# Masks, identity and turning matrices made on the chip, one-pass mask products, products of zeros first, and a new stored order

## The chip, the cores and the metric

The kernel runs on one core of one Trainium2 chip. The metric is the time of one execution on the device in microseconds. Durations and waits come from one profiled execution.

## The reference

Two parts follow each other for 8 batches of 576 positions. The attention has 8 heads of 64 channels; it adds a pooled attention (q, k and v averaged over 4 neighbouring positions, 144 by 144 scores, each result repeated 4 times) and a local one (only positions less than 4 apart).

```python
q_d = q.reshape(B, H, Sd, factor, D).mean(axis=3)     # k_d, v_d alike
out_up = np.repeat(sm_attn(q_d, k_d, v_d), factor, axis=2)
mask = np.abs(pos[:, None] - pos[None, :]) < factor
scores = np.where(mask, scale * np.matmul(q, k.transpose(0, 1, 3, 2)), -1000000000.0)
out_local = np.matmul(softmax(scores), v)
x = out_up + out_local                                # (batch, 576, 512)

h = gelu_tanh(x @ w_in)                               # 512 -> 1024
u, v = h[..., :512], h[..., 512:]
v_n = (v - mean(v)) / np.sqrt(var(v) + 1e-06) * g_ln
v_s = np.einsum('ts,bsd->btd', w_sg, v_n) + b_sg[None, :, None]
out = x + (u * v_s) @ w_out
```

## The kernel before, in words

A **pair** g = 4b + p is two heads of batch b; there are 32. Everything is written as small **tasks** with short names, and one long text, ORDER (line 88), lists every task in the order in which its instructions are emitted, with the engine after a slash where there is a choice (V VectorE, A ScalarE, P GpSimd). Each engine and each DMA queue runs its own instructions strictly in that order; a task waits for the data that it reads and for the buffer that it writes. The figures beside the tasks in the code ({"T": 1.85} and such) were a planner's costs and have no effect when the kernel runs.

Buffers come from three stores (SIZES, line 195): "ps", 8 banks of PSUM; "X", 10 buffers; "R", 38 buffers. `place` (line 64) walks through ORDER and hands out the buffer that has been free longest; a task that takes a buffer waits on the chip for the last reader of its former content, which can be a store to memory.

The tasks of a pair, with their lines:
- lq, lk, lv, lw: loads of q, k, v for the pooled part and v for the local part (370 to 386), on the SP queue, one on ScalarE's.
- qs, ks, vs: sums over 4 neighbours (388 to 409). qs and ks write qd and kd.
- S (the first four pairs) or YS: the local scores. Ten windows of 64 keys for 58 queries, each a 64 by 64 product per head (line 424). For the first four pairs the mask is put in by TensorE: two products ident_sb x mask_sb (line 417) open the sum, the scores add to it. For the later pairs VectorE adds the mask (ma, mb, line 432). Y is the pooled scores (line 445).
- mx, my: maxima (454, 456, 466, 468); nx, ny: their negatives; ea, eb, ec: exponentials (484, 492); re, rc: 1/sum; np, nq: normalising (506, 509).
- T, U, t: the probabilities are transposed by products with turn_l and turn_p, permuted identities (lines 512, 521); pa, pb, pc, pe copy the result from PSUM (line 221, the copy helper).
- D: probabilities times v (573, 589); oe, od, xa, xb (554 to 596): the two parts are added into x. xh, xl, xc: x split into a high and a low part for one-pass float32r products (604 to 611).

A batch then has v, u (lines 691, 769: x times w_in), vg (GELU), vb, vp, vn (mean and variance, 721 to 740), vh, vl (split, line 760), s (the spatial product, line 769), sa, sm (bias and gate, 807, 814), gh, gl (split), o (w_out, line 769), oa (adds x) and os (store, line 848). In batch 0 v is cut by k into vk tasks. Tasks that begin with w load the weights (doubles, taken apart on the chip: wu, wq, wb, wt, wh, wl, lines 297 to 326). s0.0 is the first spatial product of batch 0; it needs vl0.0 to vl0.4 and all of w_sg (wlq).

Ahead of the tasks a few clears are emitted (line 269 to 273): qd and od on GpSimd, parts of pd on VectorE. One DMA, task **small** (line 276), brings 926 columns for 128 partitions: seven masks of 64 columns, the identity, the turning matrices and g_ln. S waits for it, and so do T, U, t, ma and the first s.

## Time and profile before

| | us |
|---|---|
| median of 3 runs | 572.92 (572.8 to 573.14) |
| the profiled execution, its own time | 573.11 |
| its span, first to last instruction | 571.3 |
| TensorE busy | 553.5 (97%), 6992 products |
| VectorE busy | 412.9 (72%) |
| ScalarE busy | 342.6 (60%) |
| GpSimd busy | 312.8 (55%) |
| read and written | 52.64 and 9.44 MB, 109 GB/s over the span |

A busy share is an average. What matters is in which stretch which engine is full, and which wait ends last there. A wait is listed under the task that waited and what released it. Records of one engine can overlap a little, so a sum of mean durations is somewhat more than the busy time.

### The profile page before, as it was taken

Reading aid. Unit: us, or ns where it says so; the run is one execution under the profiler, and the core shown is the slowest. Engines: PE = TensorE matmul, PEld = TensorE weight load, DVE = VectorE, ACT = ScalarE, POOL = GpSimd, SP = SyncE. Lnnn points to the kernel's source line nnn. Section 1 sums busy time; section 2 is a strip of 40 time slices with the busy share of each in tenths; the row PEclk is TensorE's granted clock in tenths of the full one; section 3 lists DMA queues with packets and bytes.
Section 4 is the critical chain, followed back from the end, with each engine's and each line's share of the span. In section 5 each row is a group of like instructions: output and inputs, shape, how many; then the busy total and the mean of one; then the engine's idle time right before and its main releaser. Section 6 shows DMA issues by size and latency. Waiting matters only on the chain.

```text
span 571.3 us, 17427 instructions
## 1 busy us (share of the span) xinstructions
PE 553.5 (97%) x6992; PEld 517.8 (91%) x6992; DVE 412.9 (72%) x908; ACT 342.6 (60%) x1242; POOL 312.8 (55%) x394
## 2 busy tenths in 40 slices
...
GB/s 304 328 229 374 126 205 177 158 64 86 101 24 58 106 138 102 166 3 17 142 184 204 44 3 142 136 168 1 89 23 97 165 44 1 22 1 2 84 0 104
DMA packets 30609, 63.21 MB, mean 111 GB/s; under 512 B 3520, under 2 KB 3776, under 8 KB 30528
## 3 DMA queue, kind: packets, MB, share of 16 engines
...
q8 instruction: 55, 0.90, 0.7%
q10 hardware_dynamic: 144, 0.30, 0.1%
q14 instruction: 26, 0.21, 0.1%
HBM read 52.64 MB, written 9.44 MB: 109 GB/s over the span
## 4 chain that ended last, share of the span: by engine, by line
PE 84%; DVE 5%; ACT 2%; issue 1%; DMA 1%; POOL 0%; DVEq 0%; ACTq 0%
PE ps L769 52%; PE ps L691 17%; PE ps L589 3%; PE ps L512 3%; PE ps L445 3%; PE ps L573 2%; PE ps L521 2%; PE ps L424 2%; DMA out_dram<-R 1%; DVE R L740 1%; DVE st L721 1%; DVE R L760 1%; DVE X L432 0%; DVE stats L456 0%; ACT R L221 0%
## 5 line engine op out<-in xcount | busy, mean ns | idle before, releaser
L769 PE MATMUL ps<-wsg_h,R 128*128 128x288 f32 x576 | 121.2, 298 | 0.0
L769 PE MATMUL ps<-X,weight_z 128*128 128x288 f32 x512 | 110.2, 297 | 0.0
L769 PE MATMUL ps<-R,weight_r 128*128 128x288 f32 x768 | 107.9, 297 | 1.7 <-DVE R L596 1.7
L769 PEld LDWEIGHTS ps<-R,weight_r 128*128 128x128 f32 x768 | 103.4, 188 | 2.7 <-DVE R L596 2.0
L484 ACT ACTIVATE X<-X,nb 128x64 f32<-128x64 f32 x280 | 93.5, 338 | 7.5 <-DVE nb L463 7.0
L691 PE MATMUL ps<-weight_y,X 128*128 128x512 f32 x320 | 96.7, 396 | 0.4 <-DVE R L221 0.2
L769 PEld LDWEIGHTS ps<-wsg_h,R 128*128 128x128 f32 x576 | 94.1, 188 | 0.6 <-DVE R L760 0.3
L769 PE MATMUL ps<-wsg_l,R 128*128 128x288 f32 x320 | 92.7, 296 | 0.0
L769 PEld LDWEIGHTS ps<-X,weight_z 128*128 128x128 f32 x512 | 84.5, 188 | 1.3 <-ACT R L703 0.3
L769 PE MATMUL ps<-R,weight_z 128*128 128x288 f32 x256 | 75.5, 295 | 0.0
L691 PEld LDWEIGHTS ps<-weight_y,X 128*128 128x128 f32 x320 | 58.2, 188 | 13.7 <-POOL R L319 1.3
L769 PEld LDWEIGHTS ps<-wsg_l,R 128*128 128x128 f32 x320 | 60.3, 189 | 0.0
L807 DVE SCALAR_TENSOR_TENSOR vs<-ps,small_sb,b_sb 128x288 f32<-128x288 f32 x64 | 32.3, 514 | 37.3 <-PE ps L769 35.8
L732 POOL TENSOR_TENSOR rs<-rs,nhalf 128x1 f32<-128x1 f32 (+1 forms) x40 | 25.0, 625 | 57.8 <-DVE rs L723 57.8
L484 ACT ACTIVATION_READ_ACCUMULATOR X<-X,nb 128x1 f32 x280 | 53.1, 190 | 0.0
L691 PE MATMUL ps<-weight_y,R 128*128 128x512 f32 x128 | 50.4, 394 | 1.1 <-issue 1.1
L814 POOL TENSOR_TENSOR R<-R,vs 128x288 f32<-128x288 f32 x25 | 22.0, 880 | 51.6 <-DVE vs L807 33.8
L408 POOL TENSOR_TENSOR pairs<-R 112x256 f32<-112x256 f32 x56 | 45.4, 811 | 7.2 <-DMA R<-in_v_dram 7.0
L221 ACT COPY R<-ps 128x464 f32<-128x464 f32 (+4 forms) x92 | 33.8, 407 | 25.7 <-PE ps L512 13.9
L788 ACT ACTIVATE R<-ps 128x288 f32<-128x288 f32 x64 | 24.8, 410 | 40.1 <-PE ps L769 38.3
L769 PEld LDWEIGHTS ps<-R,weight_z 128*128 128x128 f32 x256 | 48.2, 188 | 0.7
L221 ACT CAST R<-R 128x512 fp32r<-128x512 f32 (+2 forms) x38 | 24.5, 647 | 35.3 <-DVE R L814 12.6
...
## 6 DMA issues: line engine op xcount, KB each, us to landing
...
```

The costliest lines, as they stand in the source:

```text
L221: (nc.scalar.copy if e == "A" else ENG[e].tensor_copy)(**kw)
L408: ENG[e].tensor_tensor(out=pairs, in0=v[:, 0:2], in1=v[:, 2:4], op=ALU.add)
L445: nc.tensor.matmul(out=st["sdv"][n][os, cs], lhsT=qd2[par][hs, i * QC:i * QC + HD], rhs=st["kd"][hs, ks], start=True, stop=True)
L484: nc.scalar.activation(out=st["ms"][:, t, :], in_=src, func=AF.Exp, bias=st["nb"][:, t:t + 1], scale=scale, accum_out=sums[par][:, t:t + 1])
L512: nc.tensor.matmul(out=out, lhsT=st["ms"][0:LD, 2 * c:2 * c + 2, :], rhs=turn_l, is_transpose=True, start=True, stop=True)
L589: nc.tensor.matmul(out=o[i][hs, c * QB:(c + 1) * QB], lhsT=v[ks, c, hs], rhs=pt[ks, c, h ^ int(2 * c + i >= NA)], start=True, stop=True)
L691: nc.tensor.matmul(out=acc, lhsT=r32(l), rhs=r32(weights[f"y{k}"][:, 0, w]), start=(i == 0 and ks[0] == 0), stop=(i == len(ops) - 1 and ks ...
L732: nc.gpsimd.tensor_tensor(out=rs[0:n], in0=rs[0:n], in1=nhalf[0:n], op=ALU.pow)
L769: nc.tensor.matmul(out=acc[:, 0:HALF], lhsT=r32(l), rhs=r32(r), start=(first and n == 0), stop=(last and n == len(ops) - 1))
L788: nc.scalar.activation(out=us[i // 2][:, half(i)], in_=at["ps", "m", b, "u", i][:, 0:HALF], func=AF.Gelu_apprx_tanh)
L807: nc.vector.scalar_tensor_tensor(out=vsb[i], in0=at["ps", "m", b, "s", i][:, 0:HALF], scalar=g_sb[:, i // 2:i // 2 + 1], in1=b_sb[:, half( ...
L814: ENG[e].tensor_tensor(out=u[:, half(i)], in0=u[:, half(i)], in1=vsb[i], op=ALU.mult)
```

## The change

Six things change.
- small brings only g_ln (4 columns, task g). Masks, identity and turning matrices are made on the chip: cm (GpSimd, a clear and six selections by position), ci (GpSimd, a clear and one selection), cb (the inner mask copied four times), cl and cp (turning matrices copied out of the identity).
- cr writes a float32r copy of masks and identity into one R buffer, held until S3; the mask products of the first four pairs read it and are one-pass products. ma and mb read the float32 mask as before.
- Four tasks Z multiply od2[0] by itself into a PSUM bank: Z3 and Z1 (two products each) open the order on TensorE, Z2 (two) stands ahead of Y3 and Z0 (five) ahead of vk0.0. The first four see the cleared tile; by the time of Z2 and Z0 the tile holds results of od0. Nothing reads the bank.
- The clears of qd and od move from GpSimd to VectorE.
- S waits for cr, ma for cb, T for cl, U for cl and cp, t for cp, the first s for g, each instead of small.
- ORDER is a new one throughout, with other choices of engine for many tasks.

The diff; of ORDER (105 lines of it change) only the lines that the text speaks of.

```diff
-lk0/A lq0/S ks0/V qs0/V Y0 my0 ny0/A small S0 ec0 wy1 wuy1 lq1/S qs1/P wqy1/V wby1 wty1 mx0 wy0 lk1/S S1 ks1/P wqy0/A
-wby0 lk2 ks2/V mx1 lq2 qs2/P lq3 Y1 S2 my1 wuy0 wy3 wqy3/V nx0/A ea0 eb0 re0/V rc0 qs3/P ny1/V nx1/A ea1 wby3 mx2 ec1
-np0/P T0 nq0/P pa0/V U0 pb0/V pc0/V t0 pe0/V wz1 Y2 wty0 lk3 why1/V wqz1/V eb1 re1/V rc1 lk5 nq1/P wuz1 nx2/V ea2
...
-whq2/A ua0.0 vl0.0/V wlq2/V u0.1 ua0.1 vs6 YS7 ma7 vl0.4/V ec6 whr2/A ea6 qs8/P mb7 my7 mx7 ny7/A t5 s0.0 sa0.0 wbr0
...
-vg3.4 D17 oe17/A vb3.4 vp3.4 T18 lv19 pa18/A vn3.4 vh3.1/V ma20 mb20 mx20 o2.5 oa2.5 os2.2 lk25 vh3.3/A vl3.3/V od17
-nq18/V xa17 o2.6 lw24 vh3.4/V vl3.4/P eb19 u3.3 o2.0 u3.5 lk27 ea19 re19/V rc19 np19/P ua3.5 vh3.0/A ua3.3 vl3.0/V
...
+Z3 lq0/S cm cb/V Z1 lk1/S lk0/A ks0/V qs0/V ci cr/A S0 mx0 nx0/V ea0 lq1/S qs1/V Y0 my0 ny0/V ks1/P Y1 lq3 qs3/V lk2
+ks2/P S1 cl/V ec0 eb0 my1 mx1 nx1/V ny1/V ea1 cp/V ec1 re0/V lq2 qs2/P Y2 my2 lk3 wy2 wqy2/V rc0 nq0/P np0/P wby2 eb1
+lq4 qs4/V S2 mx2 nx2/A ea2 S3 ny2/V T0 pa0/V lk4 ks4/P ks3/P re1/V rc1 nq1/P np1/P wy0 wuy0 wqy0/A wuy2 wty2 U0 pb0/V
...
+od0 xa0 xb0 YS4 my4 T1 ma4 why2/V wly2/P wuz2 eb3 U1 pa1/V pb1/V mb4 pc1/V xh0/A lw1/S wly0/P wy1 wuy1 t1 Z2 pe1/A
...
+lk5 ks5/P xa1 Z0 lq6 nx4/A wqy3/A wby3 pb2/A pc2/V vk0.0 wz3 lw2 ec4 pe2/A wqz1/A wbz1 ea4 xb1 YS5 my5 eb4 np3/P U3
...
+vp0.4 vn0.4 u0.1 ua0.1 vl0.1/V vl0.2/V wlq2/V vh0.4/A vl0.4/V YS7 pe5/V whr1/A D4 wr2 wr0 lv6 vs6 ma7 mb7 mx7 ea6
+oe4/V my7 s0.0 sa0.0 eb6 re6/V s0.2 sm0.0/V ny7/V nx7/V ec7 eb7 wlr1/P sa0.2 lk12 lk11 lv8 rc6 nq6/P np6/P ea7 lq10
...
+xc4 v1.4 t8 pe8/V lq19 lq13 os0.3 va1.4/V t9 pe9/A ec10 ea10 re10/A wtr2 wur0 vj1.4 wqr0/V wbr0 v1.3 YS11 ma11 vp1.2
...
+ZEROS = (5, 2, 2, 2)
 SIZES = {"ps": 8, "X": 10, "R": 38}
...
-    small_sb = const.tile([P, 7 * KB + P + LD + 2 * QD + KT], F32, name="small_sb")
-    mask_sb = small_sb[:, 0:7 * KB].rearrange("p (t k) -> p t k", k=KB)
-    ident_sb = small_sb[:, 7 * KB:7 * KB + P]
-    turn_l = small_sb[0:LD, 7 * KB + P:7 * KB + P + LD]
-    turn_p = small_sb[0:QD, 7 * KB + P + LD:7 * KB + P + LD + 2 * QD].rearrange("p (i c) -> p i c", i=2)
-    g_sb = small_sb[:, 7 * KB + P + LD + 2 * QD:]
+    mask_sb = const.tile([P, 7, KB], F32, name="mask_sb")
+    ident_sb = const.tile([P, P], F32, name="ident_sb")
+    turn_l = const.tile([LD, LD], F32, name="turn_l")
+    turn_p = const.tile([QD, 2, QD], F32, name="turn_p")
+    g_sb = const.tile([P, KT], F32, name="g_sb")
...
     vs2 = [const.tile([P, HALF], F32, name=f"vs{i}") for i in range(2)]
     nc.vector.memset(nhalf, -0.5)
-    for t in qd2 + od2:
-        nc.gpsimd.memset(t, 0.0)
+    for t in od2 + qd2:
+        nc.vector.memset(t, 0.0)
...
-    add("small", {"S": 0.5}, lambda e: nc.sync.dma_start(out=small_sb, in_=small), mb=0.4)
+    def select(out, in_, step, base, rise, op, fill):
+        nc.gpsimd.affine_select(out=out, in_=in_, pattern=[[step, out.shape[-1]]], base=base, channel_multiplier=rise,
+                                compare_op=op, fill=fill)
+    def const_mask(e):
+        band = mask_sb[:, 1]
+        nc.gpsimd.memset(band, 0.0)
+        for h in range(2):
+            rows = band[h * KB:(h + 1) * KB]
+            select(rows, rows, 1, 0, -1, ALU.is_ge, NEG)
+            select(rows, rows, -1, 6, 1, ALU.is_ge, NEG)
+        select(mask_sb[:, 0], band, 1, -3, 0, ALU.is_ge, NEG)
+        select(mask_sb[:, 6], band, -1, S - QB * (NT - 1) + 2, 0, ALU.is_ge, NEG)
+    def const_ident(e):
+        nc.gpsimd.memset(ident_sb, 0.0)
+        select(ident_sb, ident_sb, -1, 0, 1, ALU.not_equal, 1.0)
+    def const_bands(e):
+        copy(e, out=mask_sb[:, 2:6], in_=mask_sb[:, 1:2].broadcast_to([P, 4, KB]))
+    early_c = {}
+    def const_round(e):
+        c = buf("R", "c", 0)
+        early_c["m"] = c[:, 0:7 * KB].rearrange("p (t k) -> p t k", k=KB)
+        early_c["i"] = c[:, 7 * KB:7 * KB + P]
+        copy(e, out=r32(early_c["m"]), in_=mask_sb)
+        copy(e, out=r32(early_c["i"]), in_=ident_sb)
+    def halves(n, rows):
+        return ident_sb[0:rows].rearrange("p (a q) -> p a q", a=2)[:, :, 0:n]
+    def const_turn_l(e):
+        copy(e, out=turn_l[:, 0:2 * QB].rearrange("p (a q) -> p a q", a=2), in_=halves(QB, LD))
+        copy(e, out=turn_l[:, 2 * QB:LD], in_=ident_sb[0:LD, QB:HD])
+    def const_turn_p(e):
+        copy(e, out=turn_p[:, 0, 0:2 * QC].rearrange("p (a q) -> p a q", a=2), in_=halves(QC, QD))
+        copy(e, out=turn_p[:, 1, 0:QC], in_=ident_sb[0:QD, HD:QD])
+        copy(e, out=turn_p[:, 1, QC:2 * QC], in_=ident_sb[0:QD, 0:QC])
+        copy(e, out=turn_p[:, :, 2 * QC:QD], in_=ident_sb[0:QD, QC:HD].rearrange("p (a q) -> p a q", a=1).broadcast_to([QD, 2, QD - 2 * QC]))
+    def zeros(i, n):
+        def emit(e):
+            z = buf("ps", "z", i)
+            for _ in range(n):
+                nc.tensor.matmul(out=z[:, 0:NT * QB // 2], lhsT=od2[0][:, 0:P], rhs=od2[0], start=True, stop=True)
+        return emit
+    for i, n in enumerate(ZEROS):
+        add(f"Z{i}", {"T": 0.48 * n}, zeros(i, n), takes=[("ps", "z", i)], gives=[("ps", "z", i)])
+    add("cm", {"P": 1.7}, const_mask)
+    add("ci", {"P": 0.5}, const_ident)
+    add("cb", {"A": 0.3, "V": 0.25}, const_bands, ["cm"])
+    add("cr", {"A": 0.7, "V": 0.5}, const_round, ["cb", "ci"], takes=[("R", "c", 0)])
+    add("cl", {"A": 0.3, "V": 0.25}, const_turn_l, ["ci"])
+    add("cp", {"A": 0.6, "V": 0.4}, const_turn_p, ["ci"])
+    add("g", {"S": 0.5}, lambda e: nc.sync.dma_start(out=g_sb, in_=small), mb=0.1)
...
             sp = [buf("ps", "s", g, i) for i in range(2)]
             if early:
                 for i in range(2):
-                    nc.tensor.matmul(out=sp[i][:, 0:NW[i] * KB], lhsT=ident_sb, rhs=mask_sb[:, MB[i]:MB[i] + NW[i], :],
+                    nc.tensor.matmul(out=sp[i][:, 0:NW[i] * KB], lhsT=r32(early_c["i"]), rhs=r32(early_c["m"])[:, MB[i]:MB[i] + NW[i]],
                                      start=True, stop=False, skip_group_check=True)
             for t in (0, 4, 1, 5, 2, 6, 3, 7, 8, 9) if early else (4, 5, 0, 6, 1, 7, 2, 8, 3, 9):
...
-        given = dict(takes=[("ps", "s", g, 0), ("ps", "s", g, 1)], gives=[("R", "q", g), ("R", "k", g)])
+        given = dict(takes=[("ps", "s", g, 0), ("ps", "s", g, 1)], gives=[("R", "q", g), ("R", "k", g)] + ([("R", "c", 0)] if early else []))
         if early:
-            add(N("S"), {"T": 1.85}, scores, [N("lq"), N("lk"), N("D", ahead), "small"], **given)
+            add(N("S"), {"T": 1.85}, scores, [N("lq"), N("lk"), N("D", ahead), "cr"], **given)
             add(N("Y"), {"T": 0.45}, scores_d, [N("qs"), N("ks")], **given_d)
             def both(e):
...
-            add(N("ma"), {"V": 0.35}, masked(0), [SN(), "small"], takes=[("X", "ms", g)], gives=[("ps", "s", g, 0)])
+            add(N("ma"), {"V": 0.35}, masked(0), [SN(), "cb"], takes=[("X", "ms", g)], gives=[("ps", "s", g, 0)])
         add(N("mx"), {"V": 0.95 if early else 0.8}, top, ([SN()] if early else [N("ma"), N("mb")]) + [N("nx", 2)])
...
-        add(N("T"), {"T": 0.44}, turn, [N("np"), "small"], takes=[("ps", "t", g, 1)], gives=[("X", "ms", g)])
-        add(N("U"), {"T": 0.42}, turn2, [N("np"), N("nq"), "small"], takes=[("ps", "t", g, 2)], gives=[("X", "ms", g)])
-        add(N("t"), {"T": 0.31}, turn3, [N("nq"), "small"], takes=[("ps", "t", g, 3)])
+        add(N("T"), {"T": 0.44}, turn, [N("np"), "cl"], takes=[("ps", "t", g, 1)], gives=[("X", "ms", g)])
+        add(N("U"), {"T": 0.42}, turn2, [N("np"), N("nq"), "cl", "cp"], takes=[("ps", "t", g, 2)], gives=[("X", "ms", g)])
+        add(N("t"), {"T": 0.31}, turn3, [N("nq"), "cp"], takes=[("ps", "t", g, 3)])
...
-            w = [f"wlq{s}" for s in range(NS)] + ["b", "small"] if first else []
+            w = [f"wlq{s}" for s in range(NS)] + ["b", "g"] if first else []
...
-    eye = np.eye(P, dtype=np.float32)
-    turns = [eye[:, i] for i in (np.r_[0:QB, HD:LD, QB:HD], np.r_[0:QC, HD:QD, QC:HD], np.r_[HD:QD, 0:QC, QC:HD])]
-    r = (np.arange(P) % KB)[:, None]
-    c = np.arange(KB)[None, :]
-    band = (c >= r) & (c <= r + 6)
-    first = band & (c >= 3)
-    last = band & (c < S - QB * (NT - 1) + 3)
-    m = np.stack([first, band, band, band, band, band, last], axis=1)
-    mask = np.where(m, 0.0, NEG).astype(np.float32)
...
-        "small": np.concatenate([mask.reshape(P, -1), eye] + turns + [g], axis=1),
+        "small": g,
```

More of the change, by code (lines that the diff above doesn't have):

```diff
@@ L99 @@
-vk3.1 ks6/V lq7 oe3/V od3 xa3 xb3 wlz3/V xh3/V ea5 re5/A xl3/P xc3 wlq0/P vk4.2 vk3.2 T4 wbz0 wtz0 U4 whq4/A t4 wlq4/V
-v0.0 v0.2 rc5 qs6/V wqr2/A pa4/A wbr2 nq5/P wq2 lw4 vg0.0 vb0.0 v0.4 vp0.0 lw5 wlz2/P pb4/A lw13 qs7/V pc4/A va0.4/A
-vj0.4 b wq1 pe4/A v0.1 whz0/A vg0.1 vb0.1 vp0.1 u0.6 vn0.0 wlz0/P lv6 wr3 wqr0/A v0.3 whq3/A vg0.3 vb0.3 vg0.2 vg0.4
-vb0.2 wqr1/A wlq3/P wbr1 vn0.1 vb0.4 u0.4 vp0.2 vn0.2 u0.7 wur2 ua0.4 ua0.6 wur1 np5/P vh0.1/A u0.5 ua0.5 vp0.3 vp0.4
-YS6 ma6 mb6 D4 oe4/A od4 vh0.2/A my6 lq8 xa4 mx6 xb4 vn0.4 whq1/A wlq1/V ny6/V vn0.3 T5 pa5/A vh0.0/A ua0.7 nx6/V U5
@@ new lines @@
+lk5 ks5/P xa1 Z0 lq6 nx4/A wqy3/A wby3 pb2/A pc2/V vk0.0 wz3 lw2 ec4 pe2/A wqz1/A wbz1 ea4 xb1 YS5 my5 eb4 np3/P U3
+ma5 mb5 mx5 T3 pa3/A wqz3/V xh1/V wtz2 wtz1 why1/A lv2 whz2/A wlz2/V t3 vk3.0 ny5/A ec5 xl1/V lv3 wuy3 wly1/V wty3 wz0
+D2 vk2.0 lw3 wr1 oe2/A od2 re4/A rc4 np4/P xa2 lq8 whz1/A vk1.0 vk2.1 nx5/A wqz0/A vk1.1 vk0.1 vk3.1 why3/A pb3/A wuz3
+pc3/A pe3/V qs6/P nq4/P lk6 g xb2 D3 wbz0 wbz3 wtz3 xh2/A xl2/V wuz0 vk1.2 xc2 wqr1/A wbr1 vk2.2 vk3.2 eb5 vk0.2 oe3/V
+od3 xa3 xb3 xc1 lw6 ks6/V YS6 ea5 re5/A wly3/P xh3/A xl3/V v0.1 whz3/A wlz3/V ma6 mb6 wtz0 whz0/A wlz0/P v0.2 vg0.2
```

185 lines of the change are left out of this document (92 added, 93 removed).

## The prediction

> **What bounds the kernel now.** I read first the waits of TensorE in the first 78 us, then the busy time of every engine in ten stretches cut where those waits change, then the chain of work in order of time.
>
> ```profile
> PE ps L445 <- DVE qd L391: 6.5, 1, 6.5
> PE ps L512 <- POOL X L506: 2.6, 3, 1.6
> PE ps L769 <- DVE R L596: 1.7, 1, 1.7
> ```
>
> These are the longest waits of TensorE over the span: total, times, longest. The largest is the start, 6.5 us until Y0 has its inputs. The L769 wait is the only one of them behind the first 78 us.
>
> ```profile
> 0.00:5.03 5.03, 0.00 (x0) 0.00 (x0) 0.39 (x3) 1.28 (x1) 1.16 (x8) 1.00 0.65 194
> 5.03:20.00 14.97, 11.74 (x192) 8.20 (x192) 12.56 (x29) 11.06 (x59) 9.02 (x12) 1.00 1.02 350
> 20.00:35.00 15.00, 13.02 (x393) 10.83 (x397) 14.64 (x39) 13.74 (x72) 12.09 (x11) 1.00 0.91 277
> 35.00:49.50 14.50, 12.99 (x266) 10.45 (x255) 12.92 (x27) 13.47 (x55) 11.52 (x14) 1.00 0.90 317
> 49.50:77.74 28.24, 27.75 (x327) 25.31 (x328) 27.29 (x57) 23.30 (x61) 21.71 (x22) 1.00 0.57 179
> 77.74:106.00 28.26, 28.26 (x404) 27.79 (x405) 25.47 (x54) 25.99 (x122) 22.82 (x26) 1.00 0.78 243
> 106.00:260.00 154.00, 154.00 (x2005) 144.20 (x2004) 114.45 (x259) 104.99 (x360) 88.21 (x123) 1.00 0.27 80
> 260.00:274.60 14.60, 14.18 (x192) 12.95 (x191) 10.62 (x22) 11.85 (x37) 4.17 (x8) 1.00 0.20 57
> 274.60:568.40 293.80, 291.56 (x3237) 278.03 (x3235) 194.54 (x425) 136.87 (x484) 142.08 (x175) 1.00 0.25 78
> 568.40:571.30 2.90, 0.00 (x0) 0.00 (x0) 0.00 (x0) 0.00 (x0) 0.00 (x0) 0.86 0.30 104
> ```
>
> The columns are the stretch, its length, then busy time of PE, PEld, DVE, ACT and POOL, the granted clock, the DMA share and GB/s. From 77.74 on TensorE is busy for all but 0.42 us (260 to 274.6) and 2.24 us (the next stretch: the L769 wait, and about 0.5 at the end for the last addition, which stays). So that part is TensorE's: 490.66 us with 488.0 us of work. Before 77.74 it idles 12.2 us (65.5 busy of 77.74), and there VectorE is the full engine: 67.4 us busy of the 72.7 us from 5.03 to 77.74, 27.29 of 28.24 in the last of these stretches.
>
> ```profile
> 76.49 1.21 DVE R L760
> 77.74 9.87 PE ps L769 x72
> ...
> 271.83 4.51 DMA out_dram<-R
> 276.94 6.63 PE ps L769 x48
> ```
>
> The chain says the same: at 77.74 the first spatial product of batch 0 (task s0.0) starts when VectorE ends vl0.4 (L760). Further on, a store of 4.51 us leads to the products at 276.94: the buffer of xa17 is freed by store os2.2, written just ahead of it in the order.
>
> So I write the time as **X + 488.0 + later stalls + 2.9 + 1.8**. X is the start of s0.0, 2.9 the tail behind the last addition (last stretch), 1.8 what lies around the span (573.11 profiled, 571.3 span). Before: 77.74 + 488.0 + 2.66 + 2.9 + 1.8 = 573.1. The profiled run lies 0.2 above the median of 572.92; what a measurement of this kernel can tell from no change is about 0.2%, 1.15 us.
>
> **The change: TensorE before X.** Counted from the two orders, as many tasks of each kind stand ahead of s0.0 on TensorE after as before, the four zero tasks apart.
>
> ```profile
> 6.50 1.33 PE L445 MATMUL ps<-kd,qd 64*64 64x144 f32 x16 [6.50 <-DVE qd L391]
> 7.76 2.50 PE L417 MATMUL ps<-small_sb 128*128 128x256 f32 x4
> 10.19 1.14 PE L424 MATMUL ps<-R,R 64*64 64x64 f32 x40
> 11.26 1.34 PE L417 MATMUL ps<-small_sb 128*128 128x256 f32 x4
> ...
> 15.14 0.93 PE L424 MATMUL ps<-R,R 64*64 64x64 f32 x40
> ...
> 25.13 0.81 PE L445 MATMUL ps<-kd,qd 64*64 64x144 f32 x16
> ```
>
> The two mask products of a task (256 and 384 columns) stand as four instructions in float32. In one pass I take half or less of 1.34 us, 0.4 us a task by the columns (640 against the 288 that L769 streams in about 0.13 us: 9.87 us for 72). That removes 0.9 us three times and 2.1 from the first, and Y0 and S0's products lose their slow start (1.33 and 1.14 instead of 0.81 and 0.93): some 5.5 us of work. The first mask task at 2.50 against 1.34 is a TensorE running at half speed until about 11 us, though the granted clock reads 1.00 throughout; the column doesn't show it.
>
> Z3 and Z1 are four products of 290 columns. By the slow pair (2.50 us for 640 columns) one takes 1.13, four 4.5 us, from about 1.2 (the clears that they read now run on VectorE, idle then) to 5.7; if the speed rises some 4 us after the first (6.50 to about 11 above), 5.4. Their cover is the wait for q and k, which ends at 5.03, so S0 pays about 0.4 us.
>
> [...]
>
> Z2 and Z0 are seven more, 0.61 each at full speed (1.34 by 290/640), 4.3 us. Their cover is TensorE's idle time, 12.2 us before and now with 5.5 less work. They read od2[0], which od0 has written by then, and od2 (the merge of pair 2) must wait until Z0 has read it; both stand in that order anyhow. I take nothing for them. Where the product behind a zero is ready, its cover is gone; then up to 3.0 us (Z0, ahead of vk0.0) lies on the path.
>
> All 5.5 us saved lie in front of X, where TensorE waits: they are worth only what X moves.
>
> **VectorE before X.** I counted the VectorE tasks up to vl0.4 in the two orders and gave each the mean of its row.
>
> ```profile
> L391 DVE TENSOR_REDUCE qd<-R 128x144 f32<-128x576 f32 x15 | 11.1, 740 | 0.2 <-DMA R<-in_qT_dram 0.2
> L506 DVE TENSOR_TENSOR X<-X,rc 128x640 f32<-128x640 f32 x9 | 9.9, 1095 | 0.2
> L221 DVE COPY R<-ps 128x464 f32<-128x464 f32 x4 | 2.5, 635 | 2.6 <-PE ps L512 2.6
> L608 DVE TENSOR_TENSOR R<-R,X 128x576 fp32r<-128x576 f32 x15 | 12.4, 825 | 0.1
> ```
>
> Before: 116 tasks, 74.5 us by means. After: 117 tasks, 75.8, with cb (0.4, done before 5.03) left out. Gone: two row sums net (0.74 each), two of three casts of xh, two weight casts, and the merges od4, xa4, xb4 and ma7, with small ones 5.5 us. New: np5 (1.1), xl3 (0.8), pa1 and pa2 (0.63 each), pb1, pb4 and pc1 (1.0), a wlq and a wl more (1.7), and the two turning matrices, cl and cp, two and four small copies, 1.05 by estimate from the 0.64 of 464 columns: 6.8 us. Net +1.3. Records overlap a little: 74.5 by means took 67.4 of busy time, so +1.3 is +1.2 and VectorE needs 68.6 us. It can't start its sums before q and k land, as before: **X = 5.03 + 68.6 + VectorE's waits.**
>
> ```profile
> DVE kd L391 <- DMA R<-in_kT_dram: 3.8, 1, 3.8
> DVE da L556 <- PE ps L589: 1.4, 1, 1.4
> DVE stats L466 <- PE ps L445: 1.4, 1, 1.4
> DVE nhalf L269 <- PEq L977: 0.8, 1, 0.8
> DVE stats L454 <- PE ps L424: 0.7, 1, 0.7
> DVE st L721 <- ACT R L703: 0.2, 1, 0.2
> ```
>
> Before, the waits after 5.03 are 5.3 us (72.7 less 67.4): the 1.4 at L466 for the slow Y0, the 0.7 at L454 for the slow S0, 1.4 at L556 for a D, 0.2, and 1.6 of crumbs. After, S0 starts at 5.4, runs at full speed for 1.3 and is ready at 6.7, when VectorE has just done its two sums (5.03 to 6.5): 0.2. So 2.1 goes. The wait at L556 comes from the place of one task and may return or not; half, 0.7. Waits after: 0.2 + 0.7 + 1.6 = **2.5, X = 76.1**. Bounds: 0.5 (X 74.1) and 5.3 as now (X 78.9).
>
> **The constants.** POOL makes the masks and the identity in two clears and seven selections. No row shows a selection.
>
> ```profile
> L732 POOL TENSOR_TENSOR rs<-rs,nhalf 128x1 f32<-128x1 f32 x32 | 20.1, 628 | 44.3 <-DVE rs L723 44.3
> L271 POOL MEMSET qd<- 128x160 f32 x2 | 0.4, 232 | 0.3 <-POOLq L977 0.3
> L977 POOL MEMSET const-float32-1.0<- 128x1 f32 x1 | 0.1, 98 | 0.0
> L788 ACT ACT_TABLE_LOAD x10 | 12.8, 1283 | 0.2
> ```
>
> Bounds: nine by 0.10 (0.9 us) and nine by 0.63 (5.7), from about 0.5; nearest is the 0.23 of a clear of similar size, 2.1 us, done at 2.6. The rounding copies cr on ScalarE, 0.8 by the copies above, then end near 3.5, under the wait for q and k. cr is a new wait: it needs ci from POOL and cb from VectorE; behind it on ScalarE stand only exponentials, which need S0 anyhow, and behind cm and ci on POOL ks1, whose k lands later. At the upper bound cr ends at 7.0 and S0 is 1.6 late; that is a rival. The 463 KB of small leave the SP queue from its second place, in a stretch where the DMA share is 1.02, and q and k go ahead of weights; that feeds the waits above and isn't counted again. g (2 KB) is loaded far ahead of s0.0. The exponentials and GELUs change places more often on ScalarE: five table loads instead of three up to s0.0, 2.6 us more at 1.28 each. They have 4.9 us of idle to lie in (28.24 less 23.30); without that cover they would hold back vl0.4's inputs by as much.
>
> **Later stalls.** Work on TensorE behind s0.0 is the same set. Of the 2.66 us the 1.7 comes from os2.2 ahead of xa17. In the new order no xa stands so near; but wbr0 on VectorE takes the buffer of os0.3 right behind it, and two ScalarE or VectorE tasks stand one product behind a store. With 4.51 us to land and a product or two between, each may cost 0 to 3. PSUM banks are also handed on a little faster: followed through both orders, 37 of 510 takes have less than half a microsecond of TensorE work between the task that frees the bank and the one that takes it, 21 before. I take **2.0** (the 0.5 that stays and 1.5 of stalls), bounds 0.5 and 4.5.
>
> Sum: 76.1 + 488.0 + 2.0 + 2.9 + 1.8 = **570.8**, 2.3 below the profiled run, 2.1 below the median.
>
> **Rivals.**
> - VectorE waits as long as now (slower). The tasks new on it (pa1, pa2, pb1, pb4, pc1) are copies that must wait for a transpose on TensorE, and it takes its queue in order; the L221 row has 2.6 us of wait for four. Then X = 78.9 and the stalls as before: 78.9 + 488.0 + 2.7 + 4.7 = 574.3. It decides for slower from waits of 4.1 us upward (with 2.7 of stalls). Against: the two named waits at the start lose their cause.
> - TensorE was the bound all along (much faster): work less 5.5, start 1.1 earlier, stalls 0.7 less: 573.1 - 7.3 = 565.8. Against: 12.2 us of TensorE idle ahead of X with VectorE at 27.29 of 28.24.
> - The constants come late or the zeros stand in the way (no change): S0 1.6 late, 572.4; a Z0 that bites comes out alike or up to 573.8.
> - The change may not do what it says: zeros that don't raise the speed leave S0 about 1.2 us longer, 572.0, also within this case.
>
> **How the numbers follow.** Forecast (568.5 to 571.7) 0.45; TensorE all along 0.11; no change 0.21; VectorE's waits 0.23, in which I count late stores on VectorE too. Faster 0.45 + 0.11 = 0.56, same 0.21, slower 0.23. The forecast's own bounds are 567.3 (waits 0.5, stalls 0.5) and 576.1 (5.3 and 4.5), both ends together unlikely. The range goes to **566.8**, half way into the case of TensorE, and to **575.5**, which holds VectorE's waits at 574.3 and a store's 1.2 on top.
>
> **What would show it.** Right: s0.0 near 76, released by VectorE; VectorE's waits after 5 us near 2.5 with L466 and L454 gone; mask products near 0.4; S0 ahead of Y0 near 5.4; TensorE idle ahead of s0.0 as long as now even with zeros counted as idle or more; 488 us of TensorE work behind it. Wrong: s0.0 not released by VectorE; TensorE idle of over 4 us behind s0.0; VectorE's waits at 4 us or more; selections over 0.6 us.

## The result and the profile after

The changed kernel takes 576.16 us (median of 20 runs, 574.05 to 580.85), the one before 572.80 (20 runs, 572.14 to 574.94): a ratio of 1.0057, 95% interval 1.0042 to 1.0073. It is slower by 3.4 us where 2.1 us less was forecast, and above the range. The profiled execution took 577.03 us, its span 575.0.

The stretches after, cut where the prediction cut them before (q and k now land at 5.33; columns as there):

```profile
0.00:5.33 5.33, 4.08 (x9) 2.89 (x10) 1.57 (x9) 2.05 (x3) 2.28 (x13) 1.00 0.63 184
5.33:20.00 14.67, 11.41 (x225) 9.32 (x224) 11.49 (x34) 11.03 (x64) 7.55 (x12) 0.79 1.04 374
20.00:35.00 15.00, 12.60 (x305) 10.28 (x304) 13.54 (x35) 11.72 (x57) 12.22 (x12) 0.87 0.91 273
35.00:49.50 14.50, 13.81 (x214) 11.09 (x215) 13.67 (x29) 13.91 (x54) 11.14 (x12) 1.00 1.03 331
49.50:80.74 31.24, 29.93 (x432) 27.64 (x429) 26.85 (x57) 27.77 (x73) 20.64 (x26) 1.00 0.58 181
80.74:106.00 25.26, 24.46 (x470) 23.36 (x469) 24.65 (x55) 20.65 (x97) 20.17 (x23) 1.00 0.52 146
106.00:260.00 154.00, 152.87 (x1852) 142.32 (x1854) 120.09 (x265) 109.15 (x350) 89.84 (x116) 1.00 0.29 89
260.00:572.10 312.10, 311.04 (x3525) 296.86 (x3516) 204.85 (x467) 154.98 (x537) 139.18 (x182) 1.00 0.24 76
```

The time 80.74 has to be explained. The prediction called X the start of s0.0. In before's trace s0.0 in fact begins at 75.85, and at 77.74 its last two products start, which had waited for vl0.4:

```profile
75.85 0.51 PE L769 MATMUL ps<-wsg_h,R 128*128 128x288 f32 x2
...
77.74 0.40 PE L769 MATMUL ps<-wsg_h,R 128*128 128x288 f32 x1
```

In after the task begins at 79.05 and the same two products run at 80.74, so 80.74 is what stands against 77.74. By the prediction's form: 80.74 + 488.4 of TensorE work behind (24.46 + 152.87 + 311.04) + 3.0 of stalls (491.36 less 488.4) + 2.9 of tail + 2.0 around the span = 577.0. X is 3.0 later than before and 4.6 later than forecast; the stalls are 1.0 more than forecast; the other terms came in within 0.4.

VectorE is no longer full: 26.85 of 31.24 us in the last stretch ahead of X, where before had 27.29 of 28.24. From 5.33 to 80.74 it works 65.6 us (68.6 forecast) and waits 9.9 (5.3 before, 2.5 forecast). Its longest waits up to 80.74, in total, times, longest:

```profile
DVE R L222 <- PE ps L568: 2.5, 1, 2.5
DVE X L488 <- PE ps L480: 1.8, 1, 1.8
DVE R L764 <- ACT R L222: 1.6, 1, 1.6
DVE stats L522 <- PE ps L501: 1.1, 1, 1.1
```

Three of the four are waits for TensorE: a copy that waits for the transposes of T0 (L568), masks that wait for scores, maxima that wait for pooled scores. So TensorE is late where VectorE needs it.

TensorE is also what X itself waits for. Its last wait ahead of X, and the two products that stand for X, with vl0.4 on VectorE between them:

```profile
53.08 0.72 PE L747 MATMUL ps<-weight_y,X 128*128 128x512 f32 x2 [1.31 <-ACT X L540]
...
79.66 0.68 DVE L816 TENSOR_TENSOR R<-R,R 64x512 fp32r<-64x512 f32 x1
...
80.74 0.30 PE L825 MATMUL ps<-wsg_h,R 128*128 128x288 f32 x1
```

From 53.08 on TensorE works without a pause, and vl0.4, on which those products waited in before, ends at 80.34, 0.4 us ahead of them. Up to X TensorE is busy for 71.8 us and idle for 8.9; before it was busy for 65.5 and idle for 12.2. So two of the signs that the prediction named for being wrong are there: s0.0 is not released by VectorE, and VectorE's waits are above 4 us.

TensorE's own waits over the span:

```profile
PE ps L473 <- ACT X L540: 2.0, 2, 1.2
PE ps L480 <- DVE R L367: 1.5, 1, 1.5
PE ps L747 <- ACT X L540: 1.3, 1, 1.3
...
PE ps L825 <- DVE R L652: 0.5, 1, 0.5
```

The first two are waits for a PSUM bank: S2 for banks that exponentials still read, YS4 for one that a weight task of VectorE held. Both leave TensorE thinly used, and there the granted clock, the third column from the end, falls:

```profile
11.00:12.00 1.00, 0.63 (x22) 0.44 (x14) 1.00 (x4) 1.00 (x8) 0.00 (x0) 1.00 1.06 419
12.00:13.00 1.00, 0.21 (x1) 0.19 (x1) 0.97 (x9) 1.00 (x9) 0.00 (x0) 1.00 1.06 421
13.00:14.00 1.00, 0.20 (x2) 0.03 (x1) 1.00 (x5) 1.00 (x8) 0.00 (x0) 0.90 1.04 280
14.00:15.00 1.00, 1.00 (x17) 0.67 (x21) 0.97 (x3) 1.00 (x7) 0.75 (x1) 0.50 1.08 261
...
27.00:28.00 1.00, 0.57 (x4) 0.42 (x3) 0.99 (x3) 0.62 (x5) 1.00 (x2) 0.73 1.07 397
28.00:29.00 1.00, 1.00 (x7) 0.82 (x6) 1.00 (x4) 1.00 (x2) 0.85 (x1) 0.50 1.05 330
```

It reads 0.50 from 14 to past 20 us and again from 28 to past 30; in before's trace it read 1.00 in every stretch up to the tail. A fall to 0.50 is called a closing of the clock, or of the clock gate, from here on. What that and the zeros look like in TensorE's timeline (start, length, line, operation, count):

```profile
9.71 0.56 PE L473 MATMUL ps<-R 128*128 128x256 f32 x2
...
16.08 0.90 PE L473 MATMUL ps<-R 128*128 128x256 f32 x2
...
28.80 2.25 PE L321 MATMUL ps<-od 128*128 128x290 f32 x4
...
35.29 2.62 PE L321 MATMUL ps<-od 128*128 128x290 f32 x10
```

The mask pair of S1 at 9.71 takes 0.56 us, that of S3 at 16.08 0.90. Z2 (28.80) runs at half speed, 2.25 us for four records. Z0 (35.29) runs at full speed, but TensorE has no idle time around it: it is busy for all of 30 to 40 us.

### The profile page after: what moved, and what is told of

It is laid out like the page before. It is cut to its first block, busy times and chain, and to the rows that moved or that the text cites. A ratio compares the mean times of both kernels' runs of the same rounds, so it can differ in the third digit from the quotient of the medians.

```text
span 575.0 us, 17528 instructions
## 1 busy us (share of the span) xinstructions
PE 560.2 (97%) x7006; PEld 523.8 (91%) x7006; DVE 416.7 (72%) x945; ACT 351.3 (61%) x1228; POOL 303.0 (53%) x393
## 5 line engine op out<-in xcount | busy, mean ns | idle before, releaser
L825 PE MATMUL ps<-X,weight_z 128*128 128x288 f32 x512 | 108.1, 296 | 0.2 <-ACT R L844 0.2
L747 PE MATMUL ps<-weight_y,X 128*128 128x512 f32 x320 | 98.3, 400 | 1.3 <-ACT X L540 1.3
L863 DVE SCALAR_TENSOR_TENSOR vs<-ps,g_sb,b_sb 128x288 f32<-128x288 f32 x64 | 32.3, 511 | 41.5 <-PE ps L825 36.9
L222 ACT COPY R<-ps 128x464 f32<-128x464 f32 (+4 forms) x69 | 27.0, 405 | 49.8 <-PE ps L568 19.4
L870 POOL TENSOR_TENSOR R<-R,vs 128x288 f32<-128x288 f32 x31 | 26.1, 846 | 52.7 <-DVE vs L863 32.3
L464 POOL TENSOR_TENSOR pairs<-R 112x256 f32<-112x256 f32 x56 | 43.9, 784 | 17.6 <-DMA R<-in_v_dram 16.8
L222 ACT CAST R<-R 128x576 fp32r<-128x576 f32 (+2 forms) x43 | 27.7, 646 | 40.1 <-POOL R L870 15.7
L899 DVE TENSOR_TENSOR R<-ps,R 128x288 f32<-128x288 f32 x64 | 28.0, 451 | 28.0 <-PE ps L825 28.0
```

The costliest lines, as they stand in the source:

```text
L222: (nc.scalar.copy if e == "A" else ENG[e].tensor_copy)(**kw)
L464: ENG[e].tensor_tensor(out=pairs, in0=v[:, 0:2], in1=v[:, 2:4], op=ALU.add)
L747: nc.tensor.matmul(out=acc, lhsT=r32(l), rhs=r32(weights[f"y{k}"][:, 0, w]), start=(i == 0 and ks[0] == 0), stop=(i == len(ops) - 1 and ks ...
L825: nc.tensor.matmul(out=acc[:, 0:HALF], lhsT=r32(l), rhs=r32(r), start=(first and n == 0), stop=(last and n == len(ops) - 1))
L863: nc.vector.scalar_tensor_tensor(out=vsb[i], in0=at["ps", "m", b, "s", i][:, 0:HALF], scalar=g_sb[:, i // 2:i // 2 + 1], in1=b_sb[:, half( ...
L870: ENG[e].tensor_tensor(out=u[:, half(i)], in0=u[:, half(i)], in1=vsb[i], op=ALU.mult)
```

## The experiments

Each kernel ran beside the kernel before on the same chip. The ratio is to that; the mean clock is the mean, over a kernel's runs, of the granted clock over the whole execution. Single runs of one kernel are up to 8 us apart, so differences of medians under 1 us are not read. The runs are from several chips, and before itself differs between them: 572.9 beside e1, e2, e3 and e5, 572.7 beside e4 and e6 to e12, 572.1 beside e13, e14 and e16, 572.4 beside e17 to e19. Across chips the ratios are the fairer measure.

| run | order | mask products | zeros | us (median) | ratio (95%) | mean clock |
|---|---|---|---|---|---|---|
| before | old | float32 | none | 572.0 to 572.9 | 1 | 0.999 |
| after | new | one-pass | all four | 576.2 | 1.0042 to 1.0073 | 0.995 |
| e1 | new | one-pass | first two | 573.9 | 0.9994 to 1.0042 | 0.995 |
| e8, e12 | new | one-pass | without Z0; without Z2 | 576.3; 575.7 | 1.0032 to 1.0076; 1.0028 to 1.0080 | 0.994; 0.993 |
| e9 | new | one-pass | none | 576.1 | 1.0034 to 1.0070 | 0.994 |
| e2 | new | float32 | all four | 579.8 | 1.0086 to 1.0142 | 0.994 |
| e5 | new | one-pass | all and two more | 575.4 | 1.0018 to 1.0063 | 0.998 |
| e14 | new | one-pass | first two and four more | 576.2 | 1.0043 to 1.0083 | 0.999 |
| e16 | new, sm0.2 moved | one-pass | first two | 573.0 | 0.9992 to 1.0035 | 0.995 |
| e3, e11 | old | one-pass | none | 570.3; 571.5 | 0.9931 to 0.9971; 0.9957 to 0.9990 | 0.996; 0.995 |
| e4 | old | one-pass | first two | 573.1 | 0.9990 to 1.0028 | 0.991 |
| e10 | old | one-pass | first two and one more | 573.0 | 0.9981 to 1.0028 | 0.995 |
| e13 | old | one-pass | three in waits | 572.5 | 0.9984 to 1.0030 | 0.998 |
| e7 | old | float32, made on chip | none | 572.2 | 0.9979 to 1.0001 | 0.999 |
| e6 | old, one R buffer turned | as before | none | 572.9 | 0.9995 to 1.0025 | 1.000 |
| e18 | old, lk25 moved | as before | none | 571.2 | 0.9957 to 0.9992 | 1.000 |
| e19 | old, lk25 moved | float32, made on chip | none | 570.2 | 0.9932 to 0.9971 | 0.999 |
| e17 | old, lk25 moved | one-pass | none | 570.3 | 0.9931 to 0.9975 | 0.996 |

My theory after the result was that the closing clock took the time. Its rivals: the late zeros in TensorE's way, and the new order itself.

### The late zeros

```diff
-ZEROS = (5, 2, 2, 2)
+ZEROS = (0, 2, 0, 2)
```

(The places stand for Z0, Z1, Z2, Z3; e8 is (0, 2, 2, 2), e12 (5, 2, 0, 2), e9 (0, 0, 0, 0).)

> After without its two later blocks of zeros, Z2 (2.25 us in after's profile) and Z0 (2.62 us); Z3 and Z1 at the start stay. If these blocks lie in TensorE's way, s0.0 starts up to 4.9 us earlier than after's 79.05 and the time falls to between 571.3 and 574. If the clock gate's two closures are what costs, the granted clock still falls to 0.50 at 14 us, the blocks matter little, and the time stays between 575 and 577. If it is the new order alone, 575 to 576.5 as well.

> After without Z0 alone (five products of zeros just ahead of vk0.0, 2.62 us in after's profile); Z2 stays. If Z0 stands in TensorE's way, nearly all of the 2.3 us that both late blocks cost comes back: 573.7 to 574.7. If it is Z2, which lies where the clock had closed, 575.5 to 576.3.

> After without Z2 alone (2.25 us in after's profile, at half speed); Z0 stays. Without Z0 alone the time stayed at 576.3. If Z2 is what costs, by standing in the way or by what it pushes apart behind it, this comes down to 573.5 to 574.5, as without both. If each of the two is covered as long as the other is there, or the difference between those runs is chance, 575 to 576.5.

Without both the time falls by 2.3 us, but without either alone it does not fall by more than these runs tell. The few runs whose mean clock was 0.999 or more say otherwise: 573.2 without Z0 and 573.3 without Z2 (two runs each), 575.3 for after (five). What one block costs by itself is therefore open; that both together cost is shown. The profiled run of e1 had the clock at 1.00 throughout, so it shows the new order without closings and without late zeros:

```profile
10.00:20.00 10.00, 6.89 (x193) 5.58 (x184) 9.45 (x33) 9.48 (x54) 6.36 (x9) 1.00 1.04 367
20.00:30.00 10.00, 6.88 (x193) 5.40 (x188) 9.86 (x25) 9.68 (x52) 8.33 (x8) 1.00 1.05 319
30.00:40.00 10.00, 7.87 (x225) 6.63 (x220) 9.83 (x21) 9.57 (x44) 8.80 (x10) 1.00 0.85 264
```

Here VectorE (the third busy time) is full, 9.45 to 9.86 of 10 us, and TensorE idles for 8.4 us of these 30. This is the state that the prediction described, but it ends there: from 35.28 on, after its last wait, TensorE works without a pause up to X. The last two products of s0.0 start at 75.19, against 76.1 forecast; vl0.4 ended 0.4 us earlier, at 74.77. In after the same three stretches have 7.44, 9.83 and 8.63 us of VectorE.

### No zeros at all, and the order alone

> After without any of the four blocks of zeros; the new order, constants and one-pass masks stay. In the old order the first zeros made the time longer (573.1 with, 570.3 without) although the first products then ran at full speed: warmed up early, TensorE has thin stretches at 11 to 14 us and the clock closes there. If that holds in the new order too, this is 570.5 to 572.5, below the 573.9 with the first zeros and below before, and the profile shows no stretch at 0.50 after the first 20 us. If the order itself is what costs, it stays at 573.5 or above.

That expectation fell: 576.1, as slow as after. The old order with the same constants and one-pass masks and without zeros is e3, run again as e11:

```diff
-Z3 lq0/S cm cb/V Z1 lk1/S lk0/A ks0/V qs0/V ci cr/A S0 mx0 ...
+lk0/A lq0/S cm cb/V ks0/V qs0/V ci cr/A Y0 my0 cl/A cp/A ny0/A g S0 ec0 ...
```

(the rest of the order as before)

> The order of before, with the constants made on the chip, the one-pass mask products and the small load of g, and without any zeros. If the new order costs, this is at or below before: 571 to 572.9. If the shorter mask products are what thins out TensorE and closes the gate, the granted clock falls somewhere between 10 and 30 us here too and the time is 573 to 575.5.

> The old order with the new constants and one-pass masks and no zeros once more, to see how far its gain holds from chip to chip: 569.5 to 571 if it does; 572 or more if the gain was the chance absence of the store stall at 275 us (0.4 us of idle time there in place of 1.7 to 2.1).

So with everything else alike and no zeros, the new order, its choice of engines included, costs about 5 us (576.1 against 570.3 and 571.5; e9 and e11 ran on the same chip). The first zeros win some 2 of them back (e1). In the old order the same first zeros win nothing:

```diff
-lk0/A lq0/S cm cb/V ks0/V
+Z3 lk0/A lq0/S cm cb/V Z1 ks0/V
```

> The order of before with the new constants, the one-pass masks and the two blocks of zeros ahead of everything (Z3 and Z1), no later zeros: against the run without late zeros of the new order this differs in the order alone. If the new order costs by itself, this is at least 2 us below that run's 573.9, so 568.5 to 571. If warming TensorE up shortens the start, it is below the 570.3 of the same order without zeros, by up to 2 us; if VectorE sets the start, within 0.5 us of it.

573.1: they cost about 2 us there. In that profile the clock fell to 0.50 from 14 to 16 us. Whether the closings are all of the cost was tried with three more products of zeros ahead of Y1:

```diff
             sd = [buf("ps", "d", g, i) for i in range(2)]
+            if g == 1:
+                fill(sd[1][:, 224:512], 3)
```

> The old order with the new constants and the first zeros, and three more products of 288 columns of zeros ahead of Y1, in its own second bank, where TensorE stood idle for 1.9 us and the clock closed at 13 us. If the closed clock is what made the first zeros cost 2.8 us, the granted clock is 1.00 there and the time falls to 570 to 571.5. If it is something else, it stays at 572.5 to 573.5.

573.0 and the clock closed later, at 18 and 32 us in the profiled run: inconclusive.

### Does TensorE's work count at the start?

In the new order, with the mask products back in float32:

```diff
-lhsT=r32(early_c["i"]), rhs=r32(early_c["m"])[:, MB[i]:MB[i] + NW[i]]
+lhsT=ident_sb, rhs=mask_sb[:, MB[i]:MB[i] + NW[i], :]
```

> After with the four mask products of S0 to S3 back in float32 from the masks and the identity made on the chip, and without the rounding step cr; order and zeros as in after. The products of a task take 1.34 us and more in place of 0.4, so TensorE is busier between 9 and 18 us. If the closed clock gate costs, the granted clock stays at 1.00 there and the time falls below after's 576.2, to 572.5 to 575, although TensorE's work grows by about 4 us. If the order costs, the added work shows and the time is 576 to 580.

3.6 us longer than after, though only four runs. The edit also leaves out cr and the R buffer that it held, so the turn of the buffers differs as well: that work on TensorE at the start lies on the path in the new order is likely by this run, not shown alone. In its profile the clock closed all the same, from 14.9 to 18 us; here it wasn't the short masks that closed it. In the old order the same edit, with the R buffer still taken, was e7:

> The order of before with the constants made on the chip, the R buffer taken, but the four mask products in float32 as in before. If VectorE sets the start, as the prediction has it, one-pass products are worth nothing and this is 570 to 570.8, as with them. If TensorE's work counts at the start, it is longer by up to the 3.2 us that the products grow by, 571.5 to 573.5.

572.2 against 570.3 and 571.5, but a wait behind a store differed as well, so three more runs took that wait away by moving one load, in before (e18), with the constants made on the chip (e19) and with one-pass masks too (e17):

```diff
-o2.5 oa2.5 os2.2 lk25 vh3.3/A vl3.3/V od17 nq18/V xa17 o2.6
+o2.5 oa2.5 os2.2 vh3.3/A vl3.3/V od17 nq18/V xa17 lk25 o2.6
```

> Before with the same move of lk25 and nothing else. The wait behind the store left TensorE idle for 1.7 us at 275 us in before's profile. If the wait goes and nothing else takes its place, 570.5 to 571.5; if the time comes back elsewhere, 572 to 572.8.

> The old order with the constants made on the chip, the four mask products in float32, and the same move of lk25. Against the run with one-pass masks and the same move it gives what the one-pass masks are worth in the old order, without the store wait that differed between the earlier pair. If VectorE sets the start, the two are within 1 us, as the prediction's working has it; if TensorE's work counts, this one is longer by 2 to 3 us.

> The old order with the new constants and one-pass masks, no zeros, and the load lk25 moved in the order behind the merge xa17, so that xa17 takes another buffer and no longer waits for the store os2.2 (0.8 us in the two profiles of this order so far, 2.7 to 3.1 in before and in others). The two times so far were 570.3 and 571.5. If the store wait is a part of what differs from run to run, this is 569 to 570.5, and faster than before by 2 us or more. If the gain over before was the store wait alone, this is level with before with the same move.

571.2, 570.2, 570.3, on one chip where before took 572.4: the store wait was worth about 1.2 us, the constants on the chip about 1.0 (the intervals of e18 and e19 overlap), the one-pass masks nothing that these runs tell. So in the old order TensorE's work at the start hardly counts, as the prediction has it. But the one-pass masks are not without effect: TensorE is emptier with them (busy for 7.20 us from 10 to 20 in e17's profile, for 8.40 in e19's), and its clock closes more often (a mean of 0.996 over e17's runs, 0.999 over e19's). e17:

```profile
12.00:13.00 1.00, 0.00 (x0) 0.00 (x0) 1.00 (x2) 1.00 (x8) 0.92 (x2) 1.00 1.04 401
13.00:14.00 1.00, 0.90 (x17) 0.79 (x18) 1.00 (x4) 1.00 (x9) 0.84 (x3) 0.94 1.00 326
14.00:15.00 1.00, 1.00 (x14) 0.67 (x18) 1.00 (x4) 0.97 (x8) 0.92 (x2) 0.50 1.05 400
```

And e19, with float32 masks, in the same place:

```profile
12.00:13.00 1.00, 1.00 (x41) 0.79 (x40) 0.96 (x3) 1.00 (x7) 0.87 (x2) 1.00 1.03 395
13.00:14.00 1.00, 1.00 (x21) 0.88 (x18) 1.00 (x3) 1.00 (x9) 0.89 (x2) 1.00 1.01 319
14.00:15.00 1.00, 1.00 (x4) 0.40 (x3) 1.00 (x4) 1.00 (x9) 0.86 (x2) 1.00 1.03 396
```

Of e17's twelve runs five had a mean clock of 0.999 or more, with a median of 569.2, and seven less, with 570.7; of e19's eleven of twelve, with a median of 570.0. So the one-pass masks may save up to 0.9 us where the clock stays up and lose it where it closes; differences of this size are not shown. Both e17 and e19 beat before and after; with e3 (570.3) they are the best kernels of this study.

### Holding the clock up

In the new order, products of zeros were put where TensorE waited, in e5 with the late zeros, in e14 without them, and in the old order in e13:

```diff
             sp = [buf("ps", "s", g, i) for i in range(2)]
+            if g == 2:
+                fill(sp[0][:, 0:290], 2)
...
+                if g == 4 and t == 0:
+                    fill(sp[1][:, 384:512], 4)
...
             t3 = buf("ps", "t", g, 3)
+            fill(t3[:, 0:290], 2 * (g == 0))
...
             t1 = buf("ps", "t", g, 1)
+            fill(t1[:, 0:290], {0: 1, 2: 2}.get(g, 0))
```

The first is in e5 and e14 (S2), the second in e5 (YS4), the third in e14 (t0, and two alike ahead of Y3 and vk0.0), the fourth in e13 (T0 and T2, and two alike ahead of t1). `fill(out, n)` issues n products of od2[1] by itself into out.

> After with products of zeros added in its two thin places: two of 290 columns ahead of the mask products of S2 (in its own bank, about 1.1 us) and four of 128 columns inside YS4 where it waits for its second bank (about 1.1 us). If the closing of the clock gate costs, the granted clock stays at 1.00 from 6 to 50 us, s0.0 starts at 77.5 or earlier and the time is 573 to 574.5, with little spread. If the order itself costs, the clock is 1.00 and the time is still 575.5 to 576.5. If the late zeros Z2 and Z0 cost, it is as after or longer, 576 to 578.

> After without Z2 and Z0 and with products of zeros where its profile without them showed TensorE waiting for over 1 us: two each ahead of the masks of S2, ahead of t0, ahead of Y3 and ahead of vk0.0, in the task's own bank. Without them it ran at 573.9 with a mean clock of 0.9954, and at 572.9 where the clock stayed at 0.999 and above. If the clock is what took the last 1 us, the mean clock rises to 0.998 and the median falls to 572.5 to 573.2. If what is left against the 570 of the old order is the order's later stalls, it does not fall below 572.

> The old order with the new constants and one-pass masks, no zeros at the start, and single products of zeros only where TensorE waits anyway: one ahead of the transposes of T0, two ahead of t1, two ahead of T2, each in the task's own bank. The same order without them ran at 570.3 and 571.5 with mean clocks of 0.9955 to 0.996, and its runs at 0.999 and above had a median of 569.9. If the closing clock takes the difference, the mean clock rises to 0.998 or more and the median falls to 569.5 to 570.3. If products of zeros cost what they bring, as the first zeros did, it stays at 570.5 to 572.

The mean clock came up as meant, to 0.998, 0.999 and 0.998, though in each profiled run it still closed once, and the time did not come down: 575.4, 576.2 and 572.5. e14 is even 2.3 us above e1. Its timeline says why:

```profile
18.35 1.24 PE L280 MATMUL ps<-od 128*128 128x290 f32 x4 [1.30 <-ACT X L547]
...
28.05 1.47 PE L280 MATMUL ps<-od 128*128 128x288 f32 x4 [1.34 <-DVE R L222]
...
36.25 1.22 PE L280 MATMUL ps<-od 128*128 128x290 f32 x4 [1.07 <-ACT pd L555]
```

L280 is the added product. The wait in brackets stands ahead of it, not behind it: these tasks waited for their PSUM bank, the zeros go to the same bank, so they waited as long and then ran ahead of the real work. They stood in the way for 1.2 to 1.5 us each. So these runs do not price the clock cleanly. What does, as far as it goes, is the scatter of the runs: over the 214 runs of all kernels but before, each about its own kernel's mean, 0.01 of mean clock goes with 3.1 us (a least squares fit). After's runs have a mean clock of 0.9954, before's 0.999: by that slope the clock has 1.1 of the 3.4 us. That is a correlation, not an edit of the clock alone. It agrees with the five runs of after at 0.999 or more: 575.3, still 2.5 us above before.

### The later stalls

The stretch behind X, from those last two products of s0.0 to the tail, differs little between the profiles of one order, whatever the clock did ahead of it:

| order | profiles | length, us | TensorE's work in it |
|---|---|---|---|
| old, TensorE not held up by the store os2.2 | e3, e11, e17, e18, e19 | 488.5 to 488.9 | 487.5 to 487.8 |
| old, TensorE held up by it | before, e4, e6, e7, e10, e13 | 489.4 to 490.9 | 487.8 to 488.1 |
| new | after, e1, e2, e5, e8, e9, e12, e14, e16 | 491.4 to 493.4 | 488.4 to 488.8 |

So of the 5 us that the new order costs, about 3 lie behind X, far from the start that the change is about. The profiles of e9 and e11 say the same: their spans are 4.0 us apart, of which 3.2 behind X. It is made of many small waits; after's list from X on has one of 0.5 us and six of 0.2 to 0.4, where e3's has a single one of 0.4. One of the new ones can be larger.

TensorE's stall of 1.2 us at 91 us in e1 (0.5 in after) ends when a merge on VectorE (L652) is done. VectorE's timeline there, in e1:

```profile
87.80 3.32 DVE L870 TENSOR_TENSOR R<-R,vs 128x288 f32<-128x288 f32 x1
91.04 0.45 DVE L652 TENSOR_TENSOR R<-ps,od 128x290 f32<-128x290 f32 x1
```

And GpSimd's, in e1:

```profile
86.64 1.32 POOL L375 TENSOR_TENSOR R<-R,weight_r 128x512 int32<-128x512 int32 x1
87.91 1.27 POOL L562 TENSOR_TENSOR X<-X,rc 128x640 f32<-128x640 f32 x1
89.13 0.92 POOL L565 TENSOR_TENSOR pd<-pd,rc 128x432 f32<-128x432 f32 x1
90.00 0.81 POOL L870 TENSOR_TENSOR R<-R,vs 128x288 f32<-128x288 f32 x1
```

The gate product sm0.2 on VectorE, which takes 0.6 us elsewhere (39 of its kind averaged 0.61 in before), took 3.32, as long as GpSimd ran one operation straight behind another: it ended at 91.12, 0.31 behind the last of three. The row of before:

```profile
L814 DVE TENSOR_TENSOR R<-R,vs 128x288 f32<-128x288 f32 x39 | 23.7, 610 | 1.9 <-ACT R L788 1.2
```

In after's trace the three longest of this product, 3.14, 2.48 and 1.62 us, also lie over two or more operations of GpSimd, and those that ran while GpSimd stood idle took 0.44 to 0.46. But one took 0.45 beside an operation of 2.63, so lying beside GpSimd is not enough. That GpSimd holds VectorE up is read from these rows; e16 moves this one product off VectorE:

```diff
-qs9/V sm0.2/V xa5
+qs9/V sm0.2/P xa5
```

> After without Z2 and Z0 and with one product of the gate, sm0.2, on GpSimd in place of VectorE. On VectorE it took 3.3 us at 88 us in place of 0.6, as long as GpSimd ran one operation behind the other, and the merge behind it kept the spatial product of TensorE waiting for 1.2 us. If the later stalls are what the new order costs, this stall goes and the median falls from 573.9 by about 1 us, to 572.5 to 573.2, with the clock as before. If the stall is made up for elsewhere, it stays at 573.5 to 574.3.

The stall is gone (TensorE busy for 19.93 of the 20 us from 90 to 110, against 18.78 in e1), so this product on VectorE, at that place, made it; why it took so long there is not shown by an edit. What the stall is worth is not shown either: the median is 573.0, 0.9 less, as expected, but e16 and e1 ran on different chips, before took 572.1 beside the one and 572.9 beside the other, and the ratios, 1.0013 and 1.0018, are alike.

### The wait behind a store

The store wait left TensorE idle for 1.7 us in before; in e3 VectorE waited 0.79 for the store and TensorE not at all. The first thought was that cr's R buffer had turned the buffers on, so e6 adds to before a task without instructions that takes that buffer:

```diff
+    add("c0", {"P": 0.1}, lambda e: None, takes=[("R", "c", 0)])
```

> Before, with nothing changed but the turn of the R buffers: one more buffer is taken ahead of S0 and given back by S3, as the rounding step of the change does; no instruction is added. The stall of 1.7 us at 275 us, where a merge waits for a store to free its buffer, was gone with the old order and the new constants. If the gain of that run came from this turn alone, this gives 570.5 to 571.5; if it came from the constants, 572.5 to 573.

572.9: no gain. The store wait differs between kernels of the same order: 0.79 us of VectorE in both profiles of e3's kernel, e3 and e11,

```profile
275.19 0.46 DVE L650 TENSOR_TENSOR R<-ps,od 128x290 f32<-128x290 f32 x1 [0.79 <-DMA out_dram<-R]
```

and 2.67 us in e6:

```profile
278.11 0.46 DVE L597 TENSOR_TENSOR R<-ps,od 128x290 f32<-128x290 f32 x1 [2.67 <-DMA out_dram<-R]
```

Why the same store of 288 KB lands in 2.1 us in the one and 4.0 in the other is open.

## Why the prediction was wrong

After takes 3.4 us more than before. By the runs, the constants and the one-pass masks in the old order bring 1.2 to 2.6, the store wait that TensorE lost with them included (e11 and e3, each against before beside it), the new order costs about 5 (e9 against those two), and the four blocks of zeros come to nothing together: the first two win about 2, the later two lose about as much (e9, e1, after).

- **The form X + work + stalls + tail** held: work behind X 488.4 (488.0 forecast), tail 2.9, 2.0 around the span (1.8).
- **Constants**: selections took 0.29 us each where 0.23 was taken; the last ended at 3.2, cr at 4.56 (2.6 and 3.5 forecast), still under the wait for q and k. S0 started at 4.87 (5.4). Right, and by e18 and e19 worth about 1.0 us.
- **Z3 and Z1** ended at 5.49, forecast 5.4. Right.
- **One-pass masks**: 0.4 us a task was forecast (the prediction's own figures, 640 columns against 288 in 0.137 us, give 0.3); a pair takes 0.56 at full speed, its records overlapping. "Worth only what X moves" fits the old order (e17 against e19). What the step left out is that with them the clock closed more often (mean 0.996 in e17, 0.999 in e19).
- **Z2 and Z0 "cost nothing"**: this step failed first. The cover was to be TensorE's idle time, summed over 78 us; at the places where the two blocks stand in after there was none (Z0 in a stretch of 10.00 busy of 10). Even in e1, without the blocks, TensorE waits only 1.1 us ahead of vk0.0, where Z0's 2.62 had been. Taking both out brings 2.3 us (e1). The bound of 3.0 us that the step named as the cost without cover was the right size.
- **A closing of the clock: left out, and this failed second.** The sum has no term for one, and before's trace gave no sign of it: the clock read 1.00 in every stretch up to the tail, with waits of up to 1.7 us behind the start. No wait in after was longer than 1.5 us, and the clock closed twice, the first time after TensorE was used for 0.63, 0.21 and 0.20 of three successive microseconds. That isn't a threshold: in e1 the shares in the same place were 0.37, 0.39 and 0.42, and the clock stayed up. What closes it is not shown by these runs. The runs' scatter puts its share at about 1.1 us.
- **"X = 5.03 + VectorE's work + waits"**: the form took VectorE alone to set X. The prediction's own row for 49.50 to 77.74 had TensorE busy for 27.75 of 28.24 us, more than VectorE's 27.29: nearly all of the 12.2 us of idle TensorE lay ahead of 49.5, so work behind that was work on the path. In after and e1 TensorE works without a pause from 53.08 and from 35.28 up to X, and vl0.4 is done 0.4 us before it is needed.
- **VectorE's waits of 2.5**: 9.9 in after. That this follows from the two failures above is argued from the trace; with late zeros and closings gone (e1's profile) X was 75.19, better than the 76.1 forecast. Part of that is luck: there VectorE started at 4.85, worked 66.6 us where 68.6 was forecast and waited 3.8 where 2.5 was, and the errors cancel. The rival "VectorE waits as long as now" had the sign and the mechanism: the longest new wait, 2.5 us, is a copy, now on VectorE, that waits for a transpose. Its size (5.3) was too small, since it left TensorE's speed as it was.
- **Later stalls of 2.0: too small.** 3.0 in after, 4.1 in e1. None of the three stores that I named is among them; the largest in e1 is behind a VectorE product that took 3.32 us beside GpSimd's operations (gone in e16), which no step considered, and most of the rest are short waits that the old order does not have.
- **The order as a whole**: the prediction priced it by counting tasks, and found 1.2 us more of VectorE work. By e9 against e3 and e11 it costs about 5 us without zeros. About 3 of them lie behind X in every profile of the new order; which of the many waits there costs what was not tried, but for sm0.2. The other 2 lie ahead of X, where e9's profile has three closings and one pause of 3.6 us of TensorE for which the trace shows no cause. What of these is the order's bank waits and what the clock's chance stays open.
